# Expert 0's rows numbered by themselves, the full numbering moved into blocks one and two, one PSUM pool for four

## The chip, the core and the metric

The kernel runs on one core of one Trainium2 chip. The metric is the time of one execution on the device, in microseconds (us). The core has a matrix engine (TensorE, PE in the profile, with its weight loads as PEld), three engines for elementwise work (VectorE or DVE, ScalarE or ACT, GpSimd or POOL) and a queue of transfers (SyncE, SP). Each engine works through its own instructions in order and waits on semaphores for the others.

## What is computed

Packed attention, then a mixture of experts with the two best of eight, then a feed-forward stage, in float32. Cut to its core:

```python
p_packed = sm_attn(p, k, v)            # 4 batches, 8 heads, 576 keys, 32 packed queries
x = sm_attn(q, p_packed, p_packed)     # 2304 rows of 512 once heads are joined
noisy = x @ w_gate + log1p(exp(x @ w_noise)) * noise        # 2304 x 8
top2 = np.argpartition(-noisy, 2, axis=1)[:, :2]
w = softmax(noisy[top2])
for e in range(8):
    for k in range(2):
        mask = top2[:, k] == e
        out[mask] += w[mask, k, None] * (np.maximum(x[mask] @ w1[e], 0) @ w2[e])
h = out @ w_in                          # 512 x 2048
result = (h / (1 + exp(-h))) @ w_out
```

## The kernel before

The 2304 rows are 18 tiles of 128. The attention fills them in units of one or two tiles: `packed` makes the packed keys of one batch and half of the heads, `unpacked` the rows of a unit. It ends in `xp` matmuls (L461), which give a tile's rows and, in 16 columns more, its gate logits. ScalarE and VectorE copy them from PSUM (L466, L463, L465), and SP writes the rows to a buffer `xs` in DRAM. Weights of expert 0 arrive meanwhile and are split into a high and a low half (`split`, L114): the high half on ScalarE, the low half on GpSimd (L119), later on VectorE.

The routing numbers the rows: which of them go to which expert, in which place. `route(t0, n, lg)` does that for n tiles at once. It makes the noisy logits (L479 to L494), the two best of each row (L498, L500), a one-hot of the two choices (`oh`, `ob`, L504, L507), the place of each row among those of its expert by matmuls with a triangle and with ones (`rk`, L511 to L515), and then, by two one-hots of the place's high and low part (`oc`, L528 and L530; `oa`, L535) and one more product (`ip`, L542), a table `idx` that holds for each place the row that stands there. It runs twice: for the first 11 tiles (r0), whose end frees the gather for block one of expert 0, and for the last 7 (r1). That first gather reads rows of the 11 tiles alone; the loop at L648 runs r0 in steps beside the attention that is left.

Each expert has two blocks. Block one has 2 tiles of 128 rows (matmuls of 128x256), block two 3 (128x384). A gather (`fetch`, L191) is one indirect DMA per tile on GpSimd's queue; four transposes (`tps`, L157) turn a tile, and ScalarE and VectorE split it into `xh` and `xl`. `first` (L208 to L210) makes 12 `hps` matmuls for each of eight slices f, and `second` (L219 to L221) their product with w2, into `acc`. r1 lies inside block one of expert 0: two of its steps after each f (L663). At f = 4 it is run to its end, and five gathers go out, three for block two and two for block one of expert 1 (L667); their transposes stand between the matmuls of f = 5 to 7 and behind them.

The pools say who shares PSUM: `pTr` (2 buffers) serves the transposes, `pMx` (2) the products `pp`, `xp`, `rk`, `ip`, `i4`. They close behind block one, and later pools take their place: the `hps` of block two come from another pool (`p1`).

The order of an engine's instructions is not the program's: a scheduler with a model of times sets it when the kernel is built, except where `tc.keep_in_program_order` pins an instruction.

## Time and profile before

| | us |
|---|---|
| median of 3 runs | 1004.73 |
| the runs | 1000.46, 1004.73, 1004.75 |
| the profiled execution | 994.48 |
| its span | 992.6 |
| PE busy in it | 962.6 (97%) |
| DVE, ACT, POOL busy | 447.7, 346.4, 312.8 |
| PE busy, 0 to 124 us | 104.8 |
| PE busy, 124 to 154 us | 29.3 |

[...] PE's instructions overlap: one shows a duration of 0.28 us where the next begins 0.12 later, so a run of them is measured from start to start. A releaser in brackets is what ended an engine's idle time.

### The profile page before, as it was taken

The page shows a single profiled execution, that of the slowest core. Times are in us where ns is not written, and L with a number is a line of the kernel's source. Part 1 is how long each engine was busy: PE and PEld are TensorE (multiplying, and loading weights), DVE is VectorE, ACT ScalarE, POOL GpSimd, SP SyncE. Part 2 cuts the span into 40 slices and gives each one's busy share as a digit, 9 for nine tenths or more (in the row PEclk, how much of TensorE's full clock was granted, in tenths as well). Part 3 has the DMA queues.
Part 4 walks back from the last instruction along what each step waited for, and adds up shares of the span by engine and source line. Part 5 has one row for each costly group of instructions (what it writes and reads, how often), then busy time and mean ns, then how long its engine had stood idle before and what let it go on. Part 6 is the DMA issues. An engine that isn't in the chain of part 4 may idle for free.

```text
span 992.6 us, 14383 instructions
## 1 busy us (share of the span) xinstructions
PE 962.6 (97%) x5584; PEld 825.5 (83%) x5584; DVE 447.7 (45%) x871; ACT 346.4 (35%) x631; POOL 312.8 (32%) x345
## 2 busy tenths in 40 slices
PE   6989799999999999999999999999999999999996
PEld 4767589999999999999999988888888888888885
DVE  3536763666767676676734448312212221111111
ACT  3657323443434433343423344322222222222221
POOL 2155214252424353352200127333323322222221
PEclk9979699999999999999999999999999999999999
DMA  8995223575657666665623455101011010001001
GB/s 234 249 265 165 92 86 106 183 239 179 217 187 231 191 216 215 199 222 184 193 94 118 141 174 163 54 22 43 22 51 35 23 53 1 1 1 43 0 1 46
DMA packets 82298, 122.49 MB, mean 123 GB/s; under 512 B 16432, under 2 KB 49200, under 8 KB 82224
## 3 DMA queue, kind: packets, MB, share of 16 engines
q1 hardware_dynamic: 74416, 101.05, 32.2%
q0 software_dynamic: 7520, 19.93, 6.9%
q8 instruction: 46, 0.75, 0.3%
q10 hardware_dynamic: 288, 0.52, 0.2%
q14 instruction: 28, 0.23, 0.1%
HBM read 93.17 MB, written 28.31 MB: 122 GB/s over the span
## 4 chain that ended last, share of the span: by engine, by line
PE 90%; DVE 4%; DMA 3%; ACT 1%; SPq 1%; issue 1%; DVEq 0%; ACTq 0%
PE hps L208 14%; PE hps L210 14%; PE hps L209 14%; PE acc L220 14%; PE acc L219 14%; PE acc L221 14%; PE xp L461 1%; PE s L430 1%; PE tps L157 1%; DMA vm<-in_v_dram 1%; PE s L363 1%; DMA km<-in_k_dram 1%; PE kp L352 1%; DVE rt_oa L535 1%; DMA raw<-wf_out 0%
## 5 line engine op out<-in xcount | busy, mean ns | idle before, releaser
L176 POOL DMA_INDIRECT xg<-xs,idx x120 | 126.6, 1055 | 195.5 <-DVE xturn L185 148.0
L751 POOL TENSOR_TENSOR gl<-sg,gh 128x512 fp32r<-128x512 f32 (+1 forms) x80 | 95.3, 1193 | 253.8 <-ACT gh L750 238.2
L232 ACT ACTIVATE hh<-hps 128x384 fp32r<-128x384 f32 (+1 forms) x128 | 56.1, 438 | 260.0 <-PE hps L210 256.3
L747 DVE TENSOR_TENSOR sg<-hps,sg 128x512 f32<-128x512 f32 (+1 forms) x80 | 50.7, 634 | 196.3 <-ACT sg L746 196.1
L233 DVE SCALAR_TENSOR_TENSOR hl<-hps,hh 128x384 fp32r<-128x384 f32 (+1 forms) x128 | 62.5, 488 | 122.9 <-ACT hh L232 122.3
L746 ACT ACTIVATE sg<-hps 128x512 f32<-128x512 f32 (+1 forms) x80 | 44.2, 553 | 190.2 <-PE hps L210 189.9
L750 ACT ACTIVATE gh<-sg 128x512 fp32r<-128x512 f32 (+1 forms) x80 | 47.1, 589 | 78.4 <-DVE sg L747 78.3
L737 POOL DMA_INDIRECT y<-ys,slots x36 | 36.5, 1014 | 110.7 <-DVE hl L233 72.5
L740 DVE TENSOR_SCALAR y<-y,gates 128x512 f32<-128x512 f32 x18 | 10.8, 602 | 38.2 <-DMA y<-ys,slots 38.2
L461 PE MATMUL xp<-ppBD,a2T 128*128 128x272 f32 (+1 forms) x80 | 25.5, 462 | 1.6 <-ACT xr L51 0.8
L741 DVE SCALAR_TENSOR_TENSOR y<-y,gates,y 128x512 f32<-128x512 f32 x18 | 15.7, 871 | 24.0 <-DMA y<-ys,slots 24.0
L690 DVE SCALAR_TENSOR_TENSOR t<-raw,t 128x512 int32<-128x512 int32 x32 | 22.2, 693 | 0.9
L196 POOL DMA_INDIRECT xg<-xs,idx x10 | 9.7, 969 | 40.9 <-DVE idx_f L556 19.4
L691 DVE SCALAR_TENSOR_TENSOR t<-raw,t 128x512 int32<-128x512 int32 x32 | 22.1, 691 | 0.9
L185 DVE STREAM_TRANSPOSE xturn<-xg 128x512 f32<-128x512 f32 x30 | 21.2, 707 | 2.6 <-DMA wf_in<-t 1.5
L687 ACT ACTIVATE t<-raw 128x512 f32<-128x512 f32 x32 | 21.2, 662 | 0.1
L430 PE MATMUL s<-ppT,qT 128*128 128x64 f32 x128 | 19.6, 309 | 0.0
L430 PEld LDWEIGHTS s<-ppT,qT 128*128 128x128 f32 x128 | 19.0, 227 | 0.6
L208 PE MATMUL hps<-xha,wa3h 128*128 128x256 f32 (+1 forms) x56 | 17.7, 316 | 1.8 <-DVE sg L747 1.8
L160 DVE TENSOR_TENSOR xla<-tps,xha 128x512 fp32r<-128x512 f32 x14 | 9.6, 690 | 21.1 <-ACT xha L159 21.0
L53 DVE COPY ysb<-acc 128x512 f32<-128x512 f32 x24 | 16.4, 683 | 4.8 <-PE acc L221 4.8
L352 PE MATMUL kp<-ident,km 128*128 128x128 f32 x64 | 12.0, 327 | 6.2 <-DMA km<-in_k_dram 5.8
(450 smaller groups left out, 2987.2 us busy)
## 6 DMA issues: line engine op xcount, KB each, us to landing
raw<-in_moe_w_dram SPq DMA_DIRECT2D x56, 512.0 KB, 3.9
ys<-ysb SPq DMA_DIRECT2D x40, 256.0 KB, 3.6
raw<-in_moe_w_in_dram SPq DMA_DIRECT2D x16, 512.0 KB, 4.2
raw<-in_moe_w_out_dram SPq DMA_DIRECT2D x16, 512.0 KB, 4.2
xs<-xr SPq DMA_DIRECT2D x18, 256.0 KB, 2.1
km<-in_k_dram SPq DMA_DIRECT2D x8, 512.0 KB, 7.5
vm<-in_v_dram SPq DMA_DIRECT2D x8, 512.0 KB, 7.5
qm<-in_q_dram SPq DMA_DIRECT2D x8, 512.0 KB, 7.1
```

What stands on the lines that cost most here:

```text
L176: G.indirect_dma_start(out=xg[:, g * P:(g + 1) * P], out_offset=None, in_=xs[:, :].rearrange("n (a f) -> (n a) f", a=4), in_offset=bass.In ...
L208: T.matmul(ps, wh[:, c, s], xh[:, c, :n], start=c == 0, stop=False)
L209: T.matmul(ps, wh[:, c, s], xl[:, c, :n], start=False, stop=False)
L210: T.matmul(ps, wl[:, c, s], xh[:, c, :n], start=False, stop=c == 3)
L219: T.matmul(y, hh[:, s], wh[:, f % 2, :], start=f == 0, stop=False)
L220: T.matmul(y, hh[:, s], wl[:, f % 2, :], start=False, stop=False)
L221: T.matmul(y, hl[:, s], wh[:, f % 2, :], start=False, stop=f == last)
L232: A.activation(hh, ps, AF.Relu)
L233: V.scalar_tensor_tensor(hl, ps, 0.0, hh.bitcast(F32), op0=OP.max, op1=OP.subtract)
L430: T.matmul(s2[:, :, h, :], qT[:, h, :], ppT[b, h // 4][:, h % 4], start=True, stop=True)
L747: V.tensor_tensor(sg, ps, sg, op=OP.mult)
L751: G.tensor_tensor(gl, sg, gh.bitcast(F32), op=OP.subtract)
```

## The change

`route` becomes `first_rows`, which finds the rows of expert 0 alone: a mask `m0` of one column per tile, rank matmuls of 11 columns instead of 88, and one-hots of a sixteenth to a half of the former size. Its result is `idx0`: two columns for block one from the first 11 tiles and three for block two from all 18. The numbering for all experts, `numbers`, is a function of its own. For the first 11 tiles it is written behind block two's gather and ahead of the matmuls of block one; for the last 7 it runs as `numbers_late` inside block two, one step for each f, with the gather of expert 1's rows at f = 3 and their transposes at f = 5. `pTr` gets four buffers and serves what `pMx` served. `xr` gets four buffers, `dif` moves into a buffer of the raw weights, and the low halves of wa6 and wa7 are made on VectorE in one instruction instead of four on GpSimd, pinned to their place in the program.

Lines in the orders below are those of each kernel's own file. PE, the end of block one of expert 0 and the start of block two (`hps<-xhb`), before:

```order
L221 MATMUL acc<-wa7h,hl 128x512 x2
L157 MATMUL tps<-ident,xg 128x128 x4
L219 MATMUL acc<-wa7h,hh 128x512
L220 MATMUL acc<-wa7l,hh 128x512
L219 MATMUL acc<-wa7h,hh 128x512
L220 MATMUL acc<-wa7l,hh 128x512
L221 MATMUL acc<-wa7h,hl 128x512 x2
L208 MATMUL hps<-xhb,wa0h 128x384
L209 MATMUL hps<-xlb,wa0h 128x384
```

and with the change, where `ip` 128x5 is expert 0's table from the late tiles, `rk` 128x56 belongs to numbers_late and 128x88 with 128x40 to numbers(0):

```order
L225 MATMUL acc<-wa7h,hl 128x512 x2
...
L612 MATMUL ip<-rt_oc_1766,rt_oa_1769 128x5
...
L223 MATMUL acc<-wa7h,hh 128x512
...
L225 MATMUL acc<-wa7h,hl 128x512 x2
...
L278 MATMUL rk<-sbase,ones 128x56
...
L161 MATMUL tps<-ident,xg 128x128 x12
...
L278 MATMUL rk<-sbase,ones 128x88
...
L281 MATMUL rk<-rt_ob,before 128x88
...
L312 MATMUL ip<-rt_oc_1855,rt_oa_1809 128x40
...
L212 MATMUL hps<-xhb,wa0h 128x384
```

Twelve transposes and the 34 small matmuls of the first 11 tiles' numbering now stand between block one's last matmul and block two's first one, where there was nothing.

DVE at the same place with the change, from expert 0's last index (L625) on:

```order
L625 TENSOR_SCALAR idx_102<-row_200 128x3
...
L164 TENSOR_TENSOR xlb<-tps,xhb 128x4x128 x2
L289 TENSOR_SCALAR rt_rs<-rk 128x88
...
L290 TENSOR_TENSOR rt_oh<-rt_oh,rt_rs 128x176
...
L298 TENSOR_TENSOR rt_oc_1855<-iota_hi,rt_hi_1848 128x880
...
L300 TENSOR_TENSOR rt_oc_1855<-rt_oc_1855,rowv 128x880
...
L305 TENSOR_TENSOR rt_oa_1809<-iota_lo,rt_lo_1850 128x1024 x2
L305 TENSOR_TENSOR rt_oa_1809<-iota_lo,rt_lo_1850 128x768
...
L313 TENSOR_TENSOR idx_f<-idx_f,ip 128x40
...
L267 MAX_INDEX area<-area,ny 128x8 x7
```

The whole numbering of the first 11 tiles stands behind the `rk` that it reads; before, it stood ahead of block one.

DVE at the first numbering, from the maxima to the index of block one's gather, before:

```order
L498 MAX rt_m_1345<-rt_ny_1342 128x8 x11
L500 MAX_INDEX rt_i_1346<-rt_m_1345,rt_ny_1342 128x8 x11
...
L504 TENSOR_TENSOR rt_oh_1370<-iota_81,chosen 128x176
...
L507 TENSOR_TENSOR rt_ob_1372<-rt_oh_1370 128x88
...
L518 TENSOR_SCALAR rt_rs_1388<-rk 128x88
...
L521 TENSOR_REDUCE rt_sf_1391<-rt_oh_1370 128x22
...
L528 TENSOR_TENSOR rt_oc_1452<-iota_hi,rt_hi_1392 128x880
...
L530 TENSOR_TENSOR rt_oc_1452<-rt_oc_1452,rowv 128x880
...
L535 TENSOR_TENSOR rt_oa_1451<-iota_lo,rt_lo_1394 128x768 x3
...
L544 TENSOR_TENSOR idx_f<-idx_f,ip 128x40
...
L545 TENSOR_SCALAR idx_102<-idx_f 128x2
```

and with the change:

```order
L584 MAX rt_m_1398<-rt_ny_1395 128x8 x2
...
L587 TENSOR_TENSOR rt_m_1410<-rt_ny_1395,rt_m_1398 128x11
...
L596 SCALAR_TENSOR_TENSOR rt_sf_1424<-rk,rt_m_1410 128x11
...
L602 TENSOR_TENSOR rt_oc_1432<-iota_hi,rt_hi_1425 128x55
...
L604 TENSOR_TENSOR rt_oc_1432<-rt_oc_1432,rowv 128x55
L608 TENSOR_TENSOR rt_oa_1435<-iota_lo,rt_lo_1427 128x512 x2
L608 TENSOR_TENSOR rt_oa_1435<-iota_lo,rt_lo_1427 128x384
L267 MAX_INDEX rt_i_1810<-rt_m_1398,rt_ny_1395 128x8 x7
L622 TENSOR_SCALAR few<-c 128x1
L267 MAX_INDEX rt_i_1810<-rt_m_1398,rt_ny_1395 128x8 x4
...
L615 TENSOR_SCALAR idx_102<-ip 128x2
```

The arrays of 880 and 768 columns are gone from this stretch; the index scans (L267) of the full numbering stand in it, ahead of the write of the index.

The diff, cut to what matters:

```diff
-    dif = const.tile([P, P], F32)
+    dif = raws.tile([P, 1024], F32, name="dif", tag="raw")[:, 0:P]
...
-    idx0 = const.tile([P, TA], I32)
+    idx0 = const.tile([P, TA + TB], I32)
...
-            eng.tensor_tensor(lo[:, s], src[:, s], hi[:, s].bitcast(F32), op=OP.subtract)
+            ins = eng.tensor_tensor(lo[:, s], src[:, s], hi[:, s].bitcast(F32), op=OP.subtract)
+            if M["late"] and eng is V:
+                tc.keep_in_program_order(ins)
...
+    def numbers(t0, n, tl, oas, ps, yn, m8):
+
+        i8 = tl([E], "i8", mybir.dt.uint32)
+        for i in range(n):
+            V.max_index(i8[:, i, :], m8[:, i, :], yn[:, i, :])
+        ch = chosen[:, t0:t0 + n, :]
+        V.tensor_copy(ch, i8[:, :, 0:2])
...
+        V.tensor_tensor(oh, iota8[:, None, None, :].to_broadcast([P, n, 2, E]),
...
+        ob = tl([E], "ob", BF)
+        V.tensor_tensor(ob, oh[:, :, 0, :], oh[:, :, 1, :], op=OP.add)
...
+        rk = ps([P, n, E], "rk")
+        T.matmul(rk, ones, sbase[:, None, :].to_broadcast([P, n, E]), start=True, stop=False)
...
+        T.matmul(rk, before, ob, start=False, stop=False)
+        for j in range(n - 1):
+            T.matmul(rk[:, j + 1:, :], ones, ob[:, j:j + 1, :].to_broadcast([P, n - 1 - j, E]),
...
+        V.tensor_reduce(sn, ob.rearrange("p n e -> p e n"), axis=AX.X, op=OP.add)
+        V.tensor_tensor(seen, seen, sn, op=OP.add)
+        V.tensor_copy(seen_b, seen)
+        V.tensor_scalar(rs, rk, -63.5, None, op0=OP.add)
+        V.tensor_tensor(oh, oh, rs[:, :, None, :].to_broadcast([P, n, 2, E]), op=OP.mult)
...
+        V.tensor_reduce(sf, oh, axis=AX.X, op=OP.add)
+        V.tensor_scalar(hi, sf, 1.0 / 128, MAGIC, op0=OP.mult, op1=OP.add)
...
+        oc = tl([2, E * ET], "oc2", F16)
+        V.tensor_tensor(oc, iota_hi[:, None, None, :].to_broadcast([P, n, 2, E * ET]),
+                        hi[:, :, :, None].to_broadcast([P, n, 2, E * ET]), op=OP.is_equal)
+        V.tensor_tensor(oc, oc, rowv[:, t0:t0 + n, None, None].to_broadcast([P, n, 2, E * ET]), op=OP.mult)
+        oa = {}
+        for j0 in range(0, n, 4):
...
+            t = oas(j0, j1 - j0)
+            V.tensor_tensor(t, iota_lo[:, None, None, :].to_broadcast([P, j1 - j0, 2, P]),
...
+        ip = ps([P, E * ET], "ip")
+        for j in reversed(range(n)):
+            for c in range(2):
+                T.matmul(ip, oa[j][:, c, :], oc[:, j, c, :], start=j == n - 1 and c == 0, stop=j == 0 and c == 1)
+        V.tensor_tensor(idx_f, idx_f, ip, op=OP.add)
...
+        if t0:
+            i4 = ps([P, 4, E * ET], "i4")
+            for g in range(4):
+                for a in range(4):
+                    T.matmul(i4[32 * a:32 * a + 32, g, :], ident[:, 32 * g:32 * g + 32], idx_f, start=True, stop=True,
...
+            V.tensor_reduce(most, cnt, axis=AX.X, op=OP.max)
...
+        V.tensor_scalar(slots[:, t0:t0 + n, :], rr, 0.0, float(E * CAP - 1), op0=OP.max, op1=OP.min)
...
-        pTr = ax.enter_context(tc.tile_pool(name="pTr", bufs=2, space=PSUM))
-        pMx = ax.enter_context(tc.tile_pool(name="pMx", bufs=2, space=PSUM))
+        pTr = ax.enter_context(tc.tile_pool(name="pTr", bufs=4, space=PSUM))
...
-            pp = pMx.tile([P, 64], F32, name="pp", tag="m")
+            pp = pTr.tile([P, 64], F32, name="pp", tag="tr")
...
-                xr = sb.tile([P, 512], F32, name="xr")
+                xr = sb.tile([P, 512], F32, name="xr", bufs=4)
                 for g in range(2):
-                    xp = pMx.tile([P, 272], F32, name="xp", tag="m")
...
-        def route(t0, n, lg):
+        def first_rows(t0, n, lg):
...
+            yn = ny if t0 else tl([E], "ny")
+            V.tensor_tensor(yn, sp, nzt[:, t0:t0 + n, :], op=OP.mult)
+            V.tensor_tensor(yn, yn, lg[:, :, 0:8], op=OP.add)
...
             for i in range(n):
-                V.max(m8[:, i, :], ny[:, i, :])
-            for i in range(n):
-                V.max_index(i8[:, i, :], m8[:, i, :], ny[:, i, :])
...
-            yield
...
-            rk = pMx.tile([P, n, E], F32, name="rk", tag="m")
-            T.matmul(rk, ones, sbase[:, None, :].to_broadcast([P, n, E]), start=True, stop=False)
-            T.matmul(rk, ones, seen_b[:, None, :].to_broadcast([P, n, E]), start=False, stop=False)
-            T.matmul(rk, before, ob, start=False, stop=n == 1)
...
+            kept[t0] = yn, m8
+            m0 = tl([], "m0", BF)
+            V.tensor_tensor(m0, yn[:, :, 0], m8[:, :, 1], op=OP.is_ge)
...
+            rk = pTr.tile([P, n], F32, name="rk", tag="tr")
+            T.matmul(rk, before, m0, start=True, stop=False)
...
             for j in range(n - 1):
-                T.matmul(rk[:, j + 1:, :], ones, ob[:, j:j + 1, :].to_broadcast([P, n - 1 - j, E]),
-                         start=False, stop=j == n - 2)
...
+                T.matmul(rk[:, j + 1:], ones, m0[:, j:j + 1].to_broadcast([P, n - 1 - j]), start=False, stop=j == n - 2)
+            sf, hi, hs, lo = tl([], "sf"), tl([], "hi"), tl([], "hs"), tl([], "lo")
+            V.scalar_tensor_tensor(sf, rk, -63.5, m0, op0=OP.add, op1=OP.mult)
...
-            oa = tl([2, P], "oa", F16)
-            oc = tl([2, E * ET], "oc", F16)
...
+            oc = tl([ET], "oc", F16)
+            V.tensor_tensor(oc, iota_hi[:, None, 0:ET].to_broadcast([P, n, ET]),
+                            hi[:, :, None].to_broadcast([P, n, ET]), op=OP.is_equal)
+            V.tensor_tensor(oc, oc, rowv[:, t0:t0 + n, None].to_broadcast([P, n, ET]), op=OP.mult)
+            oa = tl([P], "oa", F16)
+            for j0 in range(0, n, 4):
+                j1 = min(n, j0 + 4)
+                V.tensor_tensor(oa[:, j0:j1], iota_lo[:, None, :].to_broadcast([P, j1 - j0, P]),
+                                lo[:, j0:j1, None].to_broadcast([P, j1 - j0, P]), op=OP.is_equal)
+            ip = pTr.tile([P, ET], F32, name="ip", tag="tr")
...
-                for c in range(2):
-                    T.matmul(ip, oa[:, j, c, :], oc[:, j, c, :], start=j + c == 0, stop=j == n - 1 and c == 1)
-            if t0 + n < NT:
-                V.tensor_tensor(idx_f, idx_f, ip, op=OP.add)
-                V.tensor_scalar(idx0, idx_f[:, 0:TA], 0.0, float((t0 + n) * P - 1), op0=OP.max, op1=OP.min)
...
+                T.matmul(ip, oa[:, j, :], oc[:, j, :], start=j == 0, stop=j == n - 1)
+            yield
+            if t0 == 0:
+                V.tensor_scalar(idx0[:, 0:TA], ip[:, 0:TA], float(-MID), float(MID), op0=OP.max, op1=OP.add)
+                V.tensor_scalar(row0, ip, float(MID), None, op0=OP.add)
...
-                V.tensor_tensor(idx_f, idx_f, ip, op=OP.add)
-                V.tensor_scalar(idx, idx_f, 0.0, float(N - 1), op0=OP.max, op1=OP.min)
...
-            yield
-
+                V.tensor_tensor(row0, row0, ip, op=OP.add)
+                V.tensor_scalar(idx0[:, TA:ET], row0[:, TA:ET], 0.0, float(N - 1), op0=OP.max, op1=OP.min)
...
-        r0 = route(0, EARLY, lgs[0])
+        r0 = first_rows(0, EARLY, lgs[0])
+        r1 = first_rows(EARLY, NT - EARLY, lgs[EARLY])
...
-                        load_w2(W[0], 0, i - 4, G)
-            if slot >= START2[5] + LAG2[3]:
-                run(r0, RSTEP)
-        for _ in r0:
+                        load_w2(W[0], 0, i - 4, G if i < 6 else V)
+            if slot == START2[5] + LAG2[3] + 1:
+                for _ in r0:
+                    pass
+            if slot == START2[-1]:
+                for i in "ab":
+                    X[i] = tuple(xp_.tile([P, 4, BW], F32R, name=f"x{c}{i}", tag=f"x{c}{i}") for c in "hl")
+                for j, xg in enumerate(fetch(xs[0:EARLY * P, :], idx0, 0, TA)):
+                    transposed(plain(xg), *X["a"], j)
+        for _ in r1:
...
-        r1 = route(EARLY, NT - EARLY, lgs[EARLY])
...
+        for j, xg in enumerate(fetch(xs[:, :], idx0, TA, TB)):
+            transposed(plain(xg), *X["b"], j)
+
+        def tl(shape, nm, dt=F32):
+            return s3.tile([P, EARLY, *shape], dt, name=f"rt_{nm}", bufs=1)
+        ones2 = tl([2, P], "oa2", F16)
+        for _ in numbers(0, EARLY, tl, lambda j, n: ones2[:, j:j + n],
+                         lambda shape, nm: pTr.tile(shape, F32, name=nm, tag="tr"), *kept[0]):
+            pass
         for f in expert_block(0, 0, TA, X["a"]):
-            run(r1, 2)
-            if f == 4:
-                for _ in r1:
-                    pass
-                rows = fetch(xs[:, :], idx, TA, TB) + fetch(xs[:, :], idx, ET, TA)
-                c = pMx.tile([P, E], F32, name="c", tag="m")
...
-            if f > 4:
-                transposed(plain(rows[f - 5]), *X["b"], f - 5)
+            pass
         flush(0)
-        for j in range(TA):
-            transposed(plain(rows[TB + j]), *X["a"], j)
...
+            def numbers_late():
+
+                n = NT - EARLY
...
+                m8 = tl([E], "m8")
+                for i in range(n):
+                    V.max(m8[:, i, :], ny[:, i, :])
+                yield from numbers(EARLY, n, tl, lambda j, k: mo.tile([P, k, 2, P], F16, name="oa", tag="t64"),
+                                   lambda shape, nm: M["t"].tile(shape, F32, name=nm, tag="tr"), ny, m8)
...
+                if e == 0:
+                    for _ in range(1 if f else 2):
+                        next(routing, None)
+                    if f == 3:
+                        box["a"] = fetch(xs[:, :], idx, ET, TA)
+                    if f == 5:
+                        for j, xg in enumerate(box["a"]):
+                            transposed(plain(xg), *X["a"], j)
+                        box["a"] = []
+                elif box["a"] and f:
```

## Rows read from the trace of the kernel before

**Rows 1.** Page, part 4: chain that ended last, shares of the span by engine

```profile
PE 90%; DVE 4%; DMA 3%; ACT 1%; SPq 1%; issue 1%; DVEq 0%; ACTq 0%
```

**Rows 2.** Stretches: us, then busy PE, PEld, DVE, ACT, POOL; PE clock, DMA share, GB/s

```profile
50.00:60.00 10.00, 7.05 (x35) 6.31 (x35) 2.72 (x8) 3.55 (x8) 2.78 (x4) 0.69 1.02 245
60.00:65.00 5.00, 5.00 (x77) 3.79 (x79) 1.51 (x5) 3.45 (x6) 3.46 (x5) 0.60 0.92 262
110.00:115.00 5.00, 2.46 (x39) 1.99 (x39) 4.71 (x12) 0.80 (x2) 0.00 (x0) 0.50 0.00 0
115.00:120.00 5.00, 4.63 (x16) 2.51 (x14) 3.72 (x12) 1.97 (x5) 3.77 (x4) 0.64 0.43 129
200.00:400.00 200.00, 200.00 (x1111) 181.73 (x1110) 137.42 (x217) 77.60 (x131) 76.34 (x73) 1.00 0.66 210
```

**Rows 3.** Waits of PE, 25 to 92 us: total, times, longest; first two of six

```profile
PE ap L378 <- ACT a1T L51: 2.9, 1, 2.9
PE apr L380 <- ACT a2T L51: 0.5, 1, 0.5
...
```

**Rows 4.** Timeline of ACT: start, us, instruction, idle before and releaser

```profile
53.20 1.06 ACT L115 ACTIVATE wa0h<-raw 128x1024 fp32r<-128x1024 f32 x1 [3.31 <-DMA raw<-in_moe_w_dram]
```

**Rows 5.** Timeline of DVE, 92 to 139 us, both routings

```profile
92.27 0.17 DVE L463 TENSOR_TENSOR lg<-xp,lg 128x16 f32<-128x16 f32 x1 [0.28 <-PE xp L461]
...
93.46 0.54 DVE L488 SCALAR_TENSOR_TENSOR rt_h<-rt_h,rt_w 128x88 f32<-128x88 f32 x2
...
94.62 0.78 DVE L488 SCALAR_TENSOR_TENSOR rt_h<-rt_h,rt_w 128x88 f32<-128x88 f32 x1
...
97.53 0.84 DVE L498 MAX8 rt_m<-rt_ny 128x8 f32<-128x8 f32 x11
...
99.78 0.15 DVE L465 COPY lg<-xp 128x16 f32<-128x16 f32 x1
...
108.81 1.06 DVE L530 TENSOR_TENSOR rt_oc<-rt_oc,rowv 128x880 f16<-128x880 f16 x1
...
109.97 3.29 DVE L535 TENSOR_TENSOR rt_oa<-iota_lo,rt_lo 128x768 f16<-128x768 f16 x4
...
114.16 0.17 DVE L545 TENSOR_SCALAR idx<-idx_f 128x2 int32<-128x2 f32 x1
...
138.78 0.18 DVE L555 TENSOR_SCALAR idx<-idx_f 128x40 int32<-128x40 f32 x1
```

**Rows 6.** Timeline of POOL, 93 to 141 us

```profile
93.80 2.87 POOL L119 TENSOR_TENSOR wa6l<-raw,wa6h 128x256 fp32r<-128x256 f32 x4 [5.03 <-PE pp L389]
...
116.71 0.95 POOL L196 DMA_INDIRECT xg<-xs,idx  x1 [0.30 <-DVE lg L465]
...
139.24 0.98 POOL L196 DMA_INDIRECT xg<-xs,idx  x1 [19.43 <-DVE idx_f L556]
140.52 0.95 POOL L196 DMA_INDIRECT xg<-xs,idx  x1 [0.31 <-issue]
```

**Rows 7.** Timeline of PE, 102 to 154 us

```profile
102.60 2.18 PE L461 MATMUL xp<-ppBD,a2T 128*128 128x272 f32 x4 [0.53 <-DVE rt_rs L518]
...
120.70 1.04 PE L157 MATMUL tps<-ident,xg 128*128 128x128 f32 x8
121.57 1.08 PE L461 MATMUL xp<-ppBD,a2T 128*128 128x272 f32 x4
122.88 0.38 PE L208 MATMUL hps<-xha,wa0h 128*128 128x256 f32 x1 [0.22 <-ACT xha L159]
...
123.97 0.48 PE L209 MATMUL hps<-xla,wa0h 128*128 128x256 f32 x1
...
137.95 0.55 PE L542 MATMUL ip<-rt_oc,rt_oa 128*128 128x40 f16 x8 [0.55 <-DVE rt_oa L535]
...
140.70 0.49 PE L560 MATMUL i<-idx_f,ident 128*32 128x40 f32 x32
...
153.46 0.44 PE L208 MATMUL hps<-xhb,wa0h 128*128 128x384 f32 x1
```

## Prediction: how the sum was made ahead of the result

> **What bounds the kernel now.** First the page's chain of waits, the work that ended last by engine: TensorE (PE) holds 90% of it [rows 1]. Then the stretches: from 200 to 400 us PE is busy for every microsecond of 200 [rows 2], and the expert loop behind goes on like that, so nothing that the change does there can shorten it. What can change is the time at which PE comes to the first matmul of expert 0's block two, 153.46 us [rows 7], and the PE work behind that point. Ahead of it PE has two soft places. At 51.85 to 54.80 it waits for ScalarE, which has waited 3.31 us for a weight tile from the DMA [rows 3, 4]; the granted clock is then 0.69 and 0.60 until about 64 us, so half speed lasted some 9 us [rows 2]. From 101.5 to 118.6 lies the first routing: the clock is 0.50 from 110 to 115 and PE busy for 2.46 of those 5 us, and it is 0.64 from 115 to 120 [rows 2]. There VectorE (DVE) is the engine that ends last: from the last logits at 92.27 to the indices at 114.16 are 21.9 us [rows 5]. The waits view from 25 to 92 us, a part that the change leaves alone except for its buffers, lists six waits: one of 2.9 us for the weight tile's sake, and five of 0.5 us down to 0.2, 1.6 together [rows 3].
>
> **The sum, step by step. Route start.** In the changed order ScalarE splits wa0 behind three xr copies and copies one more xr ahead of a1T, so the 54.80 becomes 53.20 + 1.06 + about 1.0 for ppBD, xr and a1T, with queueing 55.85: +1.05. Four transposing groups that stood ahead of the last logits stand behind them: -1.9 by my count of their starts. The last logits come at about 91.4 instead of 92.27.
>
> **First numbering.** Before, 6.1 us pass from the logits to the end of the eleven MAX (98.37) [rows 5]. Some 1.4 us of that are DVE instructions drawn out while POOL splits wa6 (0.78 for one of the three L488, 0.54 for the two before the split) [rows 5, 6]; that split goes from POOL, so 4.7. Two copies of a1T come in between: +0.3. Mask and eleven rank matmuls: 1.0. Four small operations and the two on 128x55: 0.9, where 128x880 cost 1.06 each [rows 5]. The one-hot has half the columns of the 3.29 us row, so 1.65; its eleven products 0.5. The index scans, 97.53+0.84 to 99.78 = 1.4 us [rows 5], are no longer needed but stand in DVE's queue ahead of the write of the indices and cost their time partly. The indices are there at 101.6, 12.6 us earlier. Before, from the indices 8.7 us pass to the first hps matmul and 9.8 to the second, from which on they run densely [rows 5, 7]; the POOL issue, the landing and the transposes are the same, so I take 9.3: block one runs from 110.9, not 123.97. That is 13.1 us gained.
>
> **Block one.** Before it takes 153.46 - 123.97 = 29.5 us [rows 7]. Out of it go 14 ip matmuls with their wait (1.5), the rank matmuls (0.4), the index transposes (0.5) and 20 row transposes at 0.87/8 us, 2.2 [rows 7]: -4.6. Into it come the rest of the attention, which lay before it: twelve xp at 1.08/4 us, ten transposes at 0.11 [rows 7] and eight scores, 4.6, less 0.6 that lay there already; and expert 0's late rank and index matmuls, 0.5. Together 29.4, end at 140.3. Most of the 13.1 us is still there.
>
> **The transition** gives it back. In PE's order the seven late ip stand six acc matmuls (1.4 us) before the end, so they are done at 138.9. Behind them in a row, each for the one before: indices and first gather's issue 0.5 (before, 138.78 to 139.24 [rows 5, 6]); two more issues at 1.28 (139.24 to 140.52 [rows 6]); from the issue of a gather to its transposes 116.71 to 120.70 = 4.0 [rows 6, 7]: 145.9. Four transposes 0.6 and twelve rank matmuls, about 0.6: 147.1. Then all of numbers(0) on DVE, because PE's order has its 22 ip ahead of block two: rank, multiply, reduce and small ones 1.2, oc 2 x 1.06, one-hot 3.29 [rows 5], and small ones between, 6.8: 153.9. The 22 ip 1.3 and the add to idx_f 0.3: 155.5. Before it was 153.46 without any gap: **+2.0**. PE idles some 12 us there, between 140.3 and 155.5, with only transposes and 34 small matmuls. Before, the whole DVE chain of the late tiles lay beside block one's matmuls, which cost PE only the 0.55 us of one wait [rows 7]: that cover is gone for numbers(0).
>
> **Clock.** No row shows what PE is granted after an idle stretch of this length in front of dense work. The nearest are the 2.94 us wait, after which half speed lasted 9 us [rows 2, 3], and the routing, after which it rose 4.6 us after PE had become dense at 114.01 [rows 2]. At half speed four xp cost 2.18 against 1.08 [rows 7], so half of the time is lost: 2.3 to 4.6 us, I take 3.4. The lower end of all is nothing, if the 34 small matmuls kept the clock up; the clock of 0.50 at 110 to 115, with as many small matmuls, speaks against that [rows 2]. [...]
>
> **Work moved behind.** numbers_late runs inside block two: 7 rank matmuls 0.4, 14 ip 0.9, the index transposes 0.5, and expert 1's eight row transposes 0.9 [rows 7]. PE is full there, so all of it counts: **+2.6**. DVE, half busy there, has 8 us more to do in 29 us and covers it; POOL's gathers for expert 1 start some 10 us before they are needed.
>
> **Nothing or little:** wa6 and wa7 on DVE, 1.2 us each by the other splits, fall into block one beside PE; the buffers of xr and dif; the shared PSUM buffers, at most the 1.6 us of the five short waits [rows 3].
>
> Sum: +2.0 + 3.4 + 2.6 = **+8.0 us**. The profiled execution took 994.48 us (span 992.6), the median of the runs is 1004.73; the difference lies in the long dense part, so I add to the median: **1012.7 us**.
>
> [...]
>
> **Rivals.** *Same.* The sum is right in its parts and its soft terms fall to the low side together: the route starts 1.5 us earlier through the four PSUM buffers, the clock costs 2.3, block one takes 1 us less: +8.0 - 1.5 - 1.1 - 1.0 = +4.4, 1009; with the clock kept up as well +2, 1007. *Faster.* The early start of block one is kept, because the transition is short: the late tiles' indices, and with them the gather, come before block one's end by the time that a gather needs. The place is the seven late ip. Their one-hot waits for the last xp, which stand in PE's order after 60 of 96 hps; if PE runs that stretch in the gathers' shade and the landing takes 2 us rather than 4, with the one-hots at the rate of 0.73 us for what I priced at 1.06, the gap closes by 4 to 5 us. It turns the sign where the transition is 8 us shorter than I have it, and reaches -5 where block one starts 5 us earlier besides: 998. Against it stands the order: ranks behind transposes, ip behind ranks, block two behind ip, with no other PE work between. *Slower still.* ScalarE's split of wa6 stands ahead of xr copies and waits for its raw tile, whose buffer is held by POOL's split of wa3; a wait like the 3.31 us [rows 4] would then delay the logits, and half speed as after it would cost up to 4.6: +8.0 + 3.3 + 1.2 + 2 = about +14, 1019. *It doesn't do what it says:* the first numbering is no shorter because DVE's queue holds other waits ahead of it; block one then starts at 118 or so and everything behind 7 us later: 1020, of small chance, since the removed operations are visibly on that chain.
>
> **How the numbers follow.** Forecast as worked out, slower by over 0.5% (5.0 us, about what a measurement of this kernel can tell from no change): 0.50; the same 0.30; slower still 0.10, not as it says 0.03; faster 0.07. The range goes from 1001, which leaves out most of the faster case and the edge of the same, to 1019. Slower 0.63, same 0.30, faster 0.07.
>
> **What would show it.** Right: indices for block one near 101 to 102 and its matmuls dense from 111; a PE gap of 10 to 14 us before the first 128x384 hps, released by DVE's one-hots, with a granted clock of about 0.5 behind it; that hps at 153 to 158. Wrong: a first hps of block two before 150, or a clock of 1.00 throughout, or PE waits inside block two for ranks or one-hots (which would make it slower still).

## The result, and the profile after

| | before | changed |
|---|---|---|
| median, us | 1004.73 | 1014.75 |
| runs | 5, 1000.46 to 1006.95 | 5, 1012.13 to 1017.37 |
| profiled execution (span) | 994.48 (992.6) | 1017.37 (1015.5) |
| first matmul of block one | 122.88 | 116.62 |
| first matmul of block two | 153.46 | 164.31 |
| first matmul of expert 1 | 182.79 | 197.72 |

The ratio is 1.0112, interval [1.0088, 1.0136]: slower by 10.0 us. The profiles lie further apart than the medians, because the profiled execution of the changed kernel is the longest of its five and that of before is shorter than all its timed runs; the last section tells what before was spared.

The two changed stretches do what they were written for. VectorE's and GpSimd's timeline at the first numbering (start, us, instruction, idle before and releaser), where [rows 5] and [rows 6] show the same steps before:

```profile
95.00 0.17 DVE L549 TENSOR_TENSOR lg<-xp,lg 128x16 f32<-128x16 f32 x1
...
102.07 1.82 DVE L608 TENSOR_TENSOR rt_oa<-iota_lo,rt_lo 128x512 f16<-128x512 f16 x3
...
105.45 0.15 DVE L615 TENSOR_SCALAR idx<-ip 128x2 int32<-128x2 f32 x1
```

```profile
106.52 1.16 POOL L200 DMA_INDIRECT xg<-xs,idx  x1 [4.25 <-issue]
```

and the first gather before:

```profile
115.25 1.15 POOL L196 DMA_INDIRECT xg<-xs,idx  x1 [6.89 <-PE s L437]
```

From the logits to the index are 10.4 us where [rows 5] have 21.9, and the first gather goes out 8.7 us earlier although this execution's logits came 2.7 us later. Block one starts 6.3 us earlier than [rows 7], and its last matmul still ends 6.1 us earlier (147.33 against 153.44). The 17.0 us from there to block two take all of that and 10.9 us more. TensorE's timeline between the blocks, where [rows 7] have no gap:

```profile
148.01 0.19 PE L278 MATMUL rk<-sbase,ones 128*128 128x56 bf16 x1 [0.69 <-ACT ysb L51]
...
151.17 1.08 PE L161 MATMUL tps<-ident,xg 128*128 128x128 f32 x4 [2.95 <-DMA xg<-xs,idx]
...
153.06 1.98 PE L161 MATMUL tps<-ident,xg 128*128 128x128 f32 x8 [0.82 <-DMA xg<-xs,idx]
...
154.99 0.59 PE L283 MATMUL rk<-rt_ob,ones 128*128 128x80 bf16 x10
163.02 0.91 PE L312 MATMUL ip<-rt_oc,rt_oa 128*128 128x40 f16 x22 [7.44 <-DVE rt_oa L305]
164.31 0.66 PE L212 MATMUL hps<-xhb,wa0h 128*128 128x384 f32 x1 [0.38 <-DVE idx_f L313]
```

TensorE waits first for the gather's landing (2.95 and 0.82 us), then for VectorE's whole numbering (7.44 us); all its waits there are 12.3 us. The same in stretches (us, then busy PE, PEld, DVE, ACT, POOL; granted clock, where 1.00 is the full one, DMA share, GB/s):

```profile
145.00:150.00 5.00, 2.54 (x19) 1.62 (x17) 1.35 (x4) 0.98 (x2) 2.79 (x3) 1.00 0.30 98
150.00:155.00 5.00, 3.01 (x15) 2.40 (x16) 0.84 (x2) 1.19 (x2) 0.08 (x1) 0.62 0.50 166
155.00:160.00 5.00, 0.58 (x13) 0.49 (x10) 4.85 (x15) 0.60 (x1) 0.00 (x0) 0.50 0.00 0
160.00:165.00 5.00, 1.60 (x24) 1.51 (x25) 4.09 (x16) 0.00 (x0) 0.00 (x0) 0.50 0.00 0
165.00:170.00 5.00, 5.00 (x21) 5.00 (x21) 2.84 (x25) 0.70 (x2) 0.00 (x0) 0.67 0.00 0
```

TensorE is busy for 7.73 of 20 us, and the granted clock is 0.50 from 155 us until 168.3, 4.0 us into block two: up to there its hps of 128x384, from the second on, begin 0.32 us apart, and then 0.17. From 165 to 200 us the waits view lists nothing: no rank and no one-hot is waited for in block two.

### The profile page after: what moved, and what is told of

It is laid out like the page before. It is cut to its first block, busy times and chain, and to the rows that moved or that the text cites. A ratio compares the mean times of both kernels' runs of the same rounds, so it can differ in the third digit from the quotient of the medians.

```text
span 1015.5 us, 14491 instructions
## 1 busy us (share of the span) xinstructions
PE 965.2 (95%) x5620; PEld 830.9 (82%) x5620; DVE 452.4 (45%) x902; ACT 346.4 (34%) x631; POOL 310.6 (31%) x337
## 4 chain that ended last, share of the span: by engine, by line
PE 88%; DMA 4%; DVE 2%; SPq 1%; POOL 1%; another core or an unknown queue 1%; issue 1%; ACT 1%; DVEq 0%; POOLq 0%; ACTq 0%
PE hps L214 14%; PE hps L212 14%; PE hps L213 14%; PE acc L223 13%; PE acc L224 13%; PE acc L225 13%; PE xp L547 2%; DMA km<-in_k_dram 2%; DMA raw<-in_moe_w_dram 1%; PE s L516 1%; PE tps L161 1%; PE s L449 1%; PE kp L438 1%; PE qp L509 1%
## 5 line engine op out<-in xcount | busy, mean ns | idle before, releaser
L180 POOL DMA_INDIRECT xg<-xs,idx x120 | 127.9, 1066 | 188.5 <-DVE xturn L189 155.2
L200 POOL DMA_INDIRECT xg<-xs,idx x10 | 10.5, 1049 | 62.0 <-DVE idx L316 32.3
L782 DVE TENSOR_SCALAR y<-y,gates 128x512 f32<-128x512 f32 x18 | 10.2, 565 | 39.5 <-DMA y<-ys,slots 39.5
L547 PE MATMUL xp<-ppBD,a2T 128*128 128x272 f32 (+1 forms) x80 | 21.7, 437 | 0.7 <-ACT a2T L51 0.7
L438 PEld LDWEIGHTS kp<-ident,km 128*128 128x128 f32 x64 | 9.5, 179 | 14.4 <-DVE iota_hi L84 5.1
L223 PE MATMUL acc<-wb6h,hh 128*128 128x512 f32 x40 | 16.0, 400 | 5.0 <-ACT hh L236 5.0
L533 POOL TENSOR_TENSOR sd<-sd,mx 128x512 f32<-128x512 f32 (+1 forms) x10 | 9.6, 960 | 34.4 <-DVE mx L459 12.3
```

The source lines that it names most:

```text
L180: G.indirect_dma_start(out=xg[:, g * P:(g + 1) * P], out_offset=None, in_=xs[:, :].rearrange("n (a f) -> (n a) f", a=4), in_offset=bass.In ...
L223: T.matmul(y, hh[:, s], wh[:, f % 2, :], start=f == 0, stop=False)
```

## The experiments

Times are medians, in us; "before" is the kernel before in the same comparison.

| run | time | before | ratio, interval |
|---|---|---|---|
| after_again | 1013.83 | 1003.36 | 1.0107 [1.0080, 1.0134] |
| num_before_fetch | 1009.21 | 1003.36 | 1.0066 [1.0041, 1.0091] |
| attention_first | 1006.91 | 1003.36 | 1.0040 [1.0017, 1.0064] |
| before_one_pool | 1010.57 | 1003.36 | 1.0070 [1.0045, 1.0094] |
| two_pools | 1004.03 | 1004.59 | 1.0012 [0.9982, 1.0042] |
| two_pools_attention_first | 1002.91 | 1004.59 | 0.9990 [0.9965, 1.0016] |
| splits_on_pool | 1016.20 | 1004.59 | 1.0149 [1.0107, 1.0191] |
| two_pools_again | 1007.00 | 1004.07 | 1.0046 [1.0025, 1.0068] |
| numbering_in_block_one | 1010.41 | 1004.07 | 1.0074 [1.0050, 1.0098] |
| two_pools_num_before_fetch | 1000.87 | 994.26 | 1.0056 [1.0043, 1.0070] |
| attention_first_numbering_late | 995.77 | 994.26 | 1.0024 [1.0009, 1.0038] |

before_again was one execution, 1001.84 (span 1000.1). The changed kernel and its forms with two pools stand in different comparisons, so their ratios to before are held against each other, not their times. Since a stop of ScalarE (last section) comes in behind expert 1's start and differs in size between kernels, the place where a kernel stands is also read at expert 1's first matmul, ahead of it: 182.79 and 182.58 in the two profiles of before.

**The two kernels again.**

> The changed kernel once more, for a second profile. Theory 1 (the transition): the first 128x384 hps of block two comes near 164 us again, behind a wait of about 7.4 us for VectorE's one-hots and half clock after it. Theory 2 (the front): the wait of 3.5 us for the raw tile of wa3 and the late logits (95.0 us) return, and they are what sets the loss. Theory 3 (a stop behind the routing): ScalarE's stop of 7.9 us near 215 us, which cost PE 5.0 us, returns in this profile too; if it does not, it is no part of the change's price.

> The kernel before once more, for a second profile. Its first profile (994.48 us) is below all of its timed runs (1000 to 1008), and is the only one of six profiles in which ScalarE does not stop for 6 to 8 us at its second split for expert 1's block two (its instruction 181). If the stop is no part of the change (theory 3 falls), it stands in this profile too, and the time is 1000 to 1008; if it is caused by the merged pool or by numbers_late, it is absent and the time is near 995.

The first matmuls of block one, block two and expert 1, in before_again and then in after_again:

```profile
120.44 0.39 PE L208 MATMUL hps<-xha,wa0h 128*128 128x256 f32 x1
153.03 0.45 PE L208 MATMUL hps<-xhb,wa0h 128*128 128x384 f32 x1
182.58 0.28 PE L208 MATMUL hps<-xha,wb0h 128*128 128x256 f32 x1
```

```profile
111.07 0.36 PE L212 MATMUL hps<-xha,wa0h 128*128 128x256 f32 x1
158.92 0.66 PE L212 MATMUL hps<-xhb,wa0h 128*128 128x384 f32 x1 [0.38 <-DVE idx_f L313]
191.52 0.28 PE L212 MATMUL hps<-xha,wb0h 128*128 128x256 f32 x1
```

In after_again the logits come at 90.45, the index at 100.89, and block one ends at 142.09. Its waits, 100 to 175 us (total, times, longest):

```profile
PE ip L312 <- DVE rt_oa L305: 7.4, 1, 7.4
PE tps L161 <- DMA xg<-xs,idx: 4.4, 3, 2.1
```

Of theory 1 the wait of 7.4 us and the half clock behind it (0.50 from 155 to 160 us) came again; block two starts at 158.92 and not near 164. What differs is the front (theory 2): in the first one ScalarE waits 3.54 us ahead of 72.43 for the raw tile of wa3, and TensorE 3.7 for the xr copy behind it, so that everything comes some 4.5 us later; in this repeat these two waits are 1.10 and 1.2. It is what the steps are held against below. The stop of theory 3 stands in before_again too and is no part of the change's price. Of the 10.3 us between the spans of the two repeats, 8.9 lie ahead of expert 1 and 0.8 in its length to expert 2 (65.7 against 64.9).

**Expert 0's table for all experts made ahead of the gather.**

```diff
-        for j, xg in enumerate(fetch(xs[:, :], idx0, TA, TB)):
-            transposed(plain(xg), *X["b"], j)
         def tl(shape, nm, dt=F32):
...
         for _ in numbers(0, EARLY, tl, lambda j, n: ones2[:, j:j + n],
...
+        for j, xg in enumerate(fetch(xs[:, :], idx0, TA, TB)):
+            transposed(plain(xg), *X["b"], j)
```

> numbers(0) written ahead of block two's gather, nothing else changed: its products then stand ahead of the gather's transposes and its VectorE work lies in the gather's shade. Theory 1: block two starts 7 to 9 us earlier than with the change, about 156 us, and the time falls by as much, to 1005 to 1008. Theory 2: the transition is bounded by the gather anyway, so at most 1 to 2 us are won and the time stays at 1012 or more. Theory 3: no difference in the transition that shows in the time beyond 2 us.

4.6 us faster than after_again, beside it in the comparison, though the two intervals overlap. The trace is clearer: from block one's last matmul to block two's first are 12.4 us instead of 16.8, and the wait for VectorE is 5.2 instead of 7.4. So the numbering's lost cover is part of the price. Expert 1 starts at 189.29, only 2.2 us earlier than in after_again, because block one starts 1.4 us later here and block two takes 0.75 us longer. The gap shrinks less than was expected, and the gathers' rows say why (GpSimd, then VectorE):

```profile
142.94 0.98 POOL L200 DMA_INDIRECT xg<-xs,idx  x1 [23.78 <-DVE idx L625]
144.23 1.66 POOL L200 DMA_INDIRECT xg<-xs,idx  x1 [0.30 <-issue]
146.20 4.20 POOL L200 DMA_INDIRECT xg<-xs,idx  x1 [0.30 <-issue]
```

```profile
146.32 3.23 DVE L305 TENSOR_TENSOR rt_oa<-iota_lo,rt_lo 128x1024 f16<-128x1024 f16 x3
```

In the changed kernel, where no one-hot runs beside them, the same three took 0.98, 0.95 and 0.95 us. Now the third ends 0.85 us behind the one-hots, and its transposes begin at 152.83, 6.6 us behind the start of the issue.

**One PSUM pool in the kernel before, nothing else.**

```diff
-        pTr = ax.enter_context(tc.tile_pool(name="pTr", bufs=2, space=PSUM))
-        pMx = ax.enter_context(tc.tile_pool(name="pMx", bufs=2, space=PSUM))
+        pTr = ax.enter_context(tc.tile_pool(name="pTr", bufs=4, space=PSUM))
...
-            pp = pMx.tile([P, 64], F32, name="pp", tag="m")
+            pp = pTr.tile([P, 64], F32, name="pp", tag="tr")
```

and so for xp, rk, ip, c and i4.

> The kernel before with the two PSUM pools merged into one of four buffers, nothing else. Theory 1: within 3 us of the kernel before, 1002 to 1007, since only five waits of 1.6 us together can go. Theory 2: the merged pool alone moves the weight wait and costs 3 us or more: 1008 to 1012.

7.2 us slower with the same work: in the kernel before, the pool alone costs that (theory 2). Nearly all of it lies ahead of ScalarE's stop, since expert 1 already starts 7.1 us later than in before_again:

```profile
127.56 0.39 PE L208 MATMUL hps<-xha,wa0h 128*128 128x256 f32 x1 [0.69 <-ACT xha L159]
189.72 0.28 PE L208 MATMUL hps<-xha,wb0h 128*128 128x256 f32 x1
```

TensorE's waits from 50 to 100 us (total, times, longest), where [rows 3], which are of 25 to 92 us, have one of 2.9 and 1.6 in five short ones:

```profile
PE tp L398 <- ACT ppBD L51: 3.7, 1, 3.7
PE kp L351 <- ACT xr L51: 1.5, 1, 1.5
PE tp L398 <- DVE px L391: 1.5, 2, 1.0
PE qp L422 <- ACT xr L51: 1.3, 1, 1.3
PE s L436 <- DVE sd L441: 1.2, 1, 1.2
PE pp L388 <- ACT a1T L51: 0.9, 2, 0.6
```

and the stretch from 50 to 95 us in it and in before_again (columns as above):

```profile
50.00:95.00 45.00, 35.41 (x388) 27.12 (x385) 20.83 (x70) 28.69 (x66) 25.15 (x40) 0.92 0.80 226
```

```profile
50.00:95.00 45.00, 41.54 (x455) 32.12 (x454) 23.93 (x78) 32.42 (x74) 26.46 (x43) 0.92 0.80 224
```

With four buffers in one rotation the scheduler builds another order, in which TensorE idles 9.6 us of these 45 instead of 3.5. Two of the waits are of the shared buffers themselves: `kp` and `qp` are transposes that read nothing of xr, so I read their waits of 1.5 and 1.3 us for the copy xr as waits for a buffer that an `xp` held. How the 6.1 us divide between the order and these waits no run shows. Logits come no later (91.21), but more of the attention is left over ahead of block one, which starts at 127.56, against 120.44 and 122.88.

**The pool undone in the changed kernel** (twice, in two comparisons): the inverse of that edit for pp, xp, rk, ip, c and the tiles of numbers(0).

> The changed kernel with pTr and pMx apart again (2 buffers each), nothing else undone. The scheduler then puts the first 11 tiles' rank matmuls between the late tiles' ip, and their 22 ip ahead of the last four transposes. Theory 1: numbers(0) lies in the gather's shade, block two starts within 13 us of block one's end instead of 17, and the time falls by 4 us or more against the changed kernel, to 1005 to 1010. Theory 2 (the merged pool costs 7 us in the front as it did in the kernel before): 7 us from that alone and 3 to 4 from the transition, 1002 to 1004. If the pools matter to neither: 1013.

> The changed kernel with two pools once more, for a second profile and more times. Its first profile had ScalarE's stop behind expert 1's block two at 4.8 us instead of 7 to 8, and PE lost 1.4 us there, where the changed kernel lost 5.5 and 5.1. If the short stop belongs to this order of instructions, it is short again, and the time stays near 1004. If it is chance, the stop is 7 us or more here, PE loses about 5, and the profile's time is near 1008.

Level with the kernel before in the first comparison, as theory 2 had it (1002 to 1004), and 0.46% above it in the second; the changed kernel is 1.07% above it in its own. Expert 1 starts at 188.05 and 183.80 instead of 191.52. A part of the way from 1013.83 to 1004.03 is ScalarE's stop, though, which is shorter in these two profiles (2.8 and 3.1 us in expert 1's block one, 7.2 in after_again): from expert 1's first matmul to expert 2's are 59.5 us in the first profile, 62.8 in the second and 65.7 in after_again. In the order, numbers(0)'s rank matmuls now stand between the late ip, ahead of block one's last products, and its 22 ip ahead of the last four transposes; with one pool all of them stand behind twelve transposes.

The two profiles show the same program 2.2 us apart in the stretch from the first late gather to block two (12.7 and 10.5). The third gather's issue and the one-hots, in two_pools:

```profile
145.18 4.20 POOL L200 DMA_INDIRECT xg<-xs,idx  x1 [0.30 <-issue]
```

```profile
145.31 3.22 DVE L305 TENSOR_TENSOR rt_oa<-iota_lo,rt_lo 128x1024 f16<-128x1024 f16 x3
```

and in two_pools_again:

```profile
143.67 0.95 POOL L200 DMA_INDIRECT xg<-xs,idx  x1 [0.30 <-issue]
```

```profile
143.80 3.22 DVE L305 TENSOR_TENSOR rt_oa<-iota_lo,rt_lo 128x1024 f16<-128x1024 f16 x3
```

Both issues begin 0.13 us ahead of the one-hots; one slips through, one is held for all of them. Why is open.

**Both repairs in one kernel:** two pools, and numbers(0) written ahead of the gather.

> Both repairs in one kernel: the transposes and the products have two PSUM buffers each, as before, and numbers(0) is written ahead of block two's gather. Theory (the price has two parts, the idle stretch ahead of block two and the order that the shared pool makes in front, and they act in different places): the first 128x384 hps of expert 0 comes 2 to 3 us earlier than in the two runs with two pools alone (154.65 and 150.88), at 149 to 151, with at most 8 us between block one's last acc and it instead of 10 to 12, and the median is 1001 to 1004, the same as or slightly under the kernel before. Rival (with two pools the index matmuls already stand ahead of the last transposes, so that nothing is left to gain): gap 10 us or more, 1004 to 1007, not to be told from two pools alone.

The rival held, in its plainest form: with two pools the scheduler builds the same order for both ways of writing, on every engine. So this is a third comparison of two_pools, and the cleanest, since no stop of ScalarE is in it: 0.56% above before, expert 1 at 187.88, 5.1 behind before, block two at 154.62 after a gap of 12.1. The third gather's issue is held again, 4.20 us. The prediction of a start at 149 to 151 and of a gap under 8 us missed. Undoing the pool so gives back about half of the loss (0.46 and 0.56% are left of 1.07%); the idle stretch remains, now bounded by the gather that lies under the one-hots.

**The attention ended ahead of block one, as before,** and the late tiles numbered inside it: with one pool (steps of r1, gather at f = 3, then numbers(0) in steps); with two pools, r1 and numbers(0) written ahead of block one's loop; and with two pools, gather and numbers(0) at f = 4. The core of the last:

```diff
         for f in expert_block(0, 0, TA, X["a"]):
-            pass
+            run(r1, 2)
+            if f == 4:
+                for _ in r1:
+                    pass
+                rows = fetch(xs[:, :], idx0, TA, TB)
+                for _ in g0:
+                    pass
+            if f > 4:
+                transposed(plain(rows[f - 5]), *X["b"], f - 5)
```

> Block one's gather written behind all of the attention, first_rows of the late tiles and numbers(0) as steps inside block one, block two's gather inside block one. Theory 1: block one starts 4 to 8 us later than with the change, but without any attention in it, and block two follows without a gap at 144 to 150 us; the time is 996 to 1003, below both kernels. Theory 2: the front's loss stays in full, 1005 or more. Theory 3: as the changed kernel, 1010 or more, if its stop is caused by numbers_late and its neighbours, which stay.

> Two pools, block one's gather behind all of the attention, numbers(0) ahead of block two's gather, both ahead of block one's loop. Theory 1: no gap of more than 3 us at the transition and block one at 115 to 120 us; expert 1 starts at 178 to 183 us and the time is 996 to 1002, below the kernel before. If the transition's loss is only moved on (ScalarE's wait for the stores of block one, 3 us, with half clock behind it): 1003 to 1007.

> Two pools; the attention ends ahead of block one, as in the kernel before; expert 0's late tiles are numbered inside block one in steps, and at f = 4 the gather of block two goes out and numbers(0) runs behind it beside f = 5 to 7. Theory (the loss is the idle stretch, and it goes when DVE's chain lies beside block one's matmuls): no gap over 2 us between the blocks, expert 0's first 128x384 hps at 148 to 152, then +2.6 us of work in block two, 999 to 1003, at or under the kernel before. Rival (DVE is full: the late chain and numbers(0) together are over 20 us of DVE in the 29 us of block one, and the gather waits behind them): a gap of 4 to 8 us comes back at the transition, with a releaser on DVE or the gather's DMA, and the time is 1005 to 1010.

The first missed the gain that was expected of it (1006.91): with one pool block one starts at 124.29, where the two with two pools have 116.12 and 116.89, and expert 1 at 192.51. The other two are the best of the changed forms, 0.10% under before, with an interval on both sides of it, and 0.24% above; neither beats it, which was expected of both. The first of them was expected at 178 to 183 us for expert 1 and starts it at 186.81, the last at

```profile
184.83 0.28 PE L212 MATMUL hps<-xha,wb0h 128*128 128x256 f32 x1
```

The 7.4 us wait is gone. Both keep xr's four buffers and the new place of dif, which no run undid by themselves; so these cost little. Block two's first hps even run inside block one (from 141.38 in the last). What is left is one wait of more than 1 us at the blocks' border, in the last (ScalarE, then TensorE):

```profile
153.34 0.87 ACT L236 ACTIVATE hh<-hps 128x384 fp32r<-128x384 f32 x2 [2.74 <-DMA ys<-ysb]
```

```profile
153.88 0.80 PE L223 MATMUL acc<-wa4h,hh 128*128 128x512 f32 x1 [3.02 <-ACT hh L236]
```

ScalarE's hh for block two waits for the store of block one's result, and TensorE for it. That this comes from tiles which take the same memory once block one's pools close is my reading; no run moved them.

**The whole numbering back in block one** (two pools; numbers(0) at f = 0, all of numbers for the late tiles up to f = 4, five gathers at f = 4, nothing in block two).

> Two pools; expert 0's rows of the first 11 tiles numbered by themselves as in the change, block one's gather behind all of the attention; the whole numbering of both parts inside block one, with one gather for block two and expert 1 behind it, as in the kernel before. Theory 1 (what was won in the first numbering is lost only because the rest stands in a gap): block one starts 4 to 7 us earlier than before, at 115 to 119 us, block two follows with a gap of 0 to 4 us at 146 to 150, expert 1 starts at 176 to 181 against 182.6, and the time is 997 to 1002, below the kernel before. If VectorE, which now has some 24 us of work in block one's 27, becomes the bound: a gap of 5 us or more and 1003 to 1007.

1010.41, above both ranges. The stretch from 125 to 145 us, columns as above:

```profile
125.00:145.00 20.00, 16.92 (x133) 13.96 (x132) 16.59 (x74) 1.63 (x5) 0.46 (x1) 0.91 0.04 9
```

VectorE is busy for 16.6 of 20 us, TensorE's ip wait 3.0 for one-hots, the last gathers go out at 144.5 to 149.6 and the last transposes of the five stand at 155.81. Block one takes 36.2 us instead of 31.0. That it is too short to cover both numberings explains a part of this at most: at the blocks' border ScalarE stands for 6.29 us with no named releaser, ahead of 151.82, and TensorE loses 2.24 us behind it, and how much earlier the gathered rows would have been ready without that stop no run shows.

**The splits of wa6 and wa7 back on GpSimd.**

```diff
-                        load_w2(W[0], 0, i - 4, G if i < 6 else V)
+                        load_w2(W[0], 0, i - 4, G)
```

> The changed kernel with the low halves of wa6 and wa7 on GpSimd again, in four instructions each. Theory 1: VectorE's operations of the first numbering that need two inputs are drawn out again while GpSimd splits, as before (0.78 against 0.27 us), so logits to indices take 11.5 to 12 us instead of 10.3 to 11.3, and as block one follows them, the time rises by 0 to 2 us: 1013 to 1016. Rival: the split was off the path, no difference.

2.4 us above after_again in medians of two comparisons, whose intervals overlap. The trace is clearer: while GpSimd splits wa6 from 94.18 to 96.98, VectorE's small operations take

```profile
93.73 1.28 DVE L574 SCALAR_TENSOR_TENSOR rt_h<-rt_h,rt_w 128x88 f32<-128x88 f32 x3
94.93 0.77 DVE L576 TENSOR_TENSOR rt_sa<-rt_sa,lg 128x88 f32<-128x88 f32 x1
```

where after_again has 0.82 and 0.24. An operation with one input is drawn out as well: L597, 128x11, takes 0.71 us beside the split of wa7, which lasts from 99.05 to 101.82, and 0.21 in after_again. Logits to index are 12.8 us against 10.4. Up to the end of the one-hots it is 3.6 us; the index scans, which this build's order has behind the index instead of ahead of it, give back 1.2. The prediction took 1.4 us for the move.

## Why the prediction was right, and where its terms were off

Direction, size (1012.7 against 1014.75 and 1013.83) and place held. TensorE's idle time between the blocks is 11.9 us in after_again and 12.3 in the first profile, where it said some 12; block two's start (158.92 and 164.31) came outside the 153 to 158 that it gave. Step by step, predicted and then measured in after_again, with before_again as before:

| step | predicted | measured |
|---|---|---|
| logits | 91.4 | 90.45 |
| logits to index | 10.2 | 10.4 |
| index to block one | 9.3 | 10.2 |
| block one starts | 110.9 | 111.07 |
| block one | 29.4 | 31.0 |
| block one's end to block two | 15.2 | 16.8 |
| block two starts | 155.5 | 158.92 |
| the same against before | +2.0 | +5.9 |
| block two longer by | 6.0 | 3.1 |
| expert 1 against before | +8.0 | +8.9 |

- **First numbering:** right within 0.2 us; 0.9 more from the index to block one took up the earlier logits. The "13.1 us gained" counts from the second hps matmul of before; from first to first it is 9.4 us between the two repeats, 6.3 between the first profiles.
- **Block one and the way to block two** were each 1.6 us too short. Block one holds 24 xp matmuls, 4.3 us from start to start, where the sum counted twelve at 3.2. Behind it the last eight transposes stand together and took 2.17 us at a granted clock of 0.50 (145 to 150 us), where the sum had 0.6 for four; and from the first rank matmul to block two are 9.5 us instead of 9.0, with one of VectorE's three xlb splits of the gathered rows (0.68 us, at 150.39) inside its numbering chain. With 0.2 at block one's start and 0.4 between the two profiles of before, "+2.0" became +5.9.
- **Clock:** 3.4 was too much. In block two hps at 0.32 us, where they take 0.17 at a granted clock of 1.00, last until 161.0 in after_again and 168.3 in the first profile, 2.1 and 4.0 us of work at half speed, so 1.0 to 2.0 us lost. The 9 us of half speed read from [rows 2, 3] were no guide to it.
- **Work moved behind:** what then remains of block two's 3.1 is 2.0, against 2.6. attention_first_numbering_late, with that work but without the gap, has expert 1 at 184.83, 2.0 behind before, and agrees.
- The errors cancel: the way to block two's start 3.9 too cheap, clock and moved work 2.9 too dear. That the total came so close is in part luck.
- **"Nothing or little: the shared PSUM buffers"** is the step that failed, in sign. The bound was read from the waits of the old order ("at most the 1.6 us of the five short waits"); with the shared pool the scheduler builds another order, and two groups of transposes wait besides (1.5 and 1.3 us), by my reading for the products' buffers. In the kernel before it costs 7.2 us by itself. The sum came out all the same because its terms were worked out on the changed order, which has the pool's effect in it: late ranks behind transposes, attention left over for block one. The price is right, but the prediction laid it all on the numbering's lost cover and moved work, and a good part (3.5, 3.6 and 7.7 of 8.9 us at expert 1's start in three profiles with two pools) goes with the pool.
- **Rivals.** "Slower still" has its mechanism in the first profile of the changed kernel, at wa3 rather than wa6: the raw tile's wait of 3.54 us. The repeat, where it is 1.10, still takes 1012.31, so it is not what makes the change slower. The rival "Faster" wanted a landing of 2 us rather than 4: from the first late gather's issue to its transposes are 3.75 us (141.36 to 145.11). Its 998 should also have been about 1000, 5 us under 1004.73.

## What to carry to other kernels

Merging two buffer pools can change the whole order where a scheduler sets it: compare the orders and time it by itself, before anything else is laid on it. A chain that is taken off one critical stretch must be put beside work that lasts as long; here 6 to 9 us won ahead of block one became an idle stretch behind it, since numbering, gather and transposes had only each other for cover. Don't lay a gather's issue on GpSimd under VectorE's long one-hots: here the cover lengthened what it covered by 3.2 us in four of the five profiles in which the issue began 0.12 to 0.13 us ahead of them.

## What the runs showed of the hardware that was not expected

**A gather's issue can be held while VectorE makes one-hots.** In four profiles (num_before_fetch, two_pools, two_pools_num_before_fetch, two_pools_attention_first) the third issue takes 4.18 to 4.20 us, 0.95 plus the 3.2 of the three one-hots that begin 0.12 to 0.13 us behind it. Begun 0.46 to 0.47 us ahead of them it took 1.04 (attention_first and attention_first_numbering_late), and 0.13 ahead, once, 0.95. What decides is open.

**A stop of ScalarE.** In expert 1's block one ScalarE stands for 7.9 us with no releaser that the profile knows. In the changed kernel and in before_again:

```profile
222.68 0.38 ACT L236 ACTIVATE hh<-hps 128x256 fp32r<-128x256 f32 x1 [7.87 <-remote]
```

```profile
207.70 0.39 ACT L232 ACTIVATE hh<-hps 128x256 fp32r<-128x256 f32 x1 [7.94 <-remote]
```

In the changed kernel TensorE loses 5.0 us by it. The other kernels of those comparisons show 2.8 to 7.9 us between 206 and 223 us, except attention_first (5.25 at 195), and behind 150 us ScalarE's waits without a named releaser add up to 34 to 63 us in them. Most of it is off the critical path: before_again has 33.7 us of them and a span that is 7.5 longer than the first profile's. In the profile on which the prediction was made (994.48) and in both of the last comparison there is none, and there the kernel before took 994.26, against 1003.36 to 1004.73 in the other comparisons. One program shows both: two_pools has 44.5 us of such waits and 59.5 us from expert 1 to expert 2, two_pools_num_before_fetch, the same order, none and 57.3. So the 10 us between the first profile and the median, which the prediction put down to "the long dense part", go along with this stop; it belongs to neither kernel, and what it is stays open. The three comparisons behind the first that show it ran on chips 11, 8 and 4, the one that doesn't on chip 7; whether it goes by the chip no run tells.
